# All nine groups of four output tiles by seven products: the last four plain tiles of a down-projection go

## The chip, the cores and the metric

One NeuronCore of a Trainium2 chip runs the kernel. The metric is the device time of one execution in microseconds (us). Engines are named as in the profile: PE is the matrix engine (PEld its weight loads), DVE the vector engine, ACT the scalar engine, POOL GpSimd, SP the sync engine, on whose queue nearly all transfers are issued.

## The reference

Attention with two kinds of windows for 8 batches of 8 heads, 576 positions of 64 values, followed by a two-layer projection with a leaky ReLU between:

```
scores = scale * q @ k^T                  # per batch and head
plain heads (0-3):    key in the last 32 positions
dilated heads (4-7):  key in the last 128 positions, every 4th
x = softmax(masked scores) @ v            # (8*576, 512) after merging the heads
h = x @ w_in                              # 512 -> 2048
g = max(0.01 * h, h)
out = g @ w_out                           # 2048 -> 512, (4608, 512) in fp32
```

## The kernel before

Operands are cast to fp16 and accumulated in fp32. The 4608 rows are worked in pairs of batches (1152 rows), each pair in three **chunks** of 384 rows. A chunk's up-projection makes 16 blocks of 128 hidden values, which ACT turns into `gt[c % 3]`. Chunk 0 belongs to batch 0, chunk 1 half to batch 0 and half to batch 1, chunk 2 to batch 1. The up-projection stands on line 1057 (blocks of 384 columns; ACT behind it on 1073), chunk 1's on line 1091 (two blocks of 192 at a time, its first half for batch 0 and its second for batch 1; ACT on 1104), and that of the last three chunks, by seven products, on line 1191.

Attention works in **visits** of two heads (dilated 2 and 3, then plain 0 and 1), two units each: scores (L899), exp on ACT (L907), sums (L924), values (L918), logarithm and reciprocal on ACT (L943, L945), normalisation on DVE into `xt` (L956). Batches 0 and 1 ("early") are loaded with long rows, cast, and transposed on PE (L743). What their first 512 positions leave over, 64 positions a head, is the **remainder**: loaded by `load_rest` into `rest`, transposed by PE (L791), and worked as a unit of its own (L993 to L1032). Batches 2 to 7 are loaded in 128-byte pieces, cast by POOL (L505), and transposed by DVE (L708, L713, L720).

The down-projection has 36 tiles of 128 rows by 512 columns. The first four (`PLAIN = 4`: the three of chunk 0 and the first of chunk 1) are plain: `down` makes each in four **parts** of four matmuls of 512 columns (L1271), evicts it with one copy (L1279) and stores it. A part needs four blocks of the chunk and four rows of `w_out`. The other 32 go through `group`, eight groups of four tiles. A group regards 2 x 2 pairs of tiles, halves of the hidden dimension and halves of the columns as a 2 x 2 block product and makes it of seven products (the Winograd form of Strassen's) instead of eight. One product is eight matmuls of 256 columns for each of two tiles (L1361). Before them DVE forms eight sums and differences of activations (`add_up`, L1347: s1 to s4, two tiles each, in the halves `rest` and `pair1` and in place in `gt`), and once for the whole kernel four of `w_out` (`weight_sums`, L1301: into the former staging buffer `wst`, into `t4`, and in place into `w_out`, this last one behind all plain parts). Between them ACT or DVE evicts or adds partial results (L1390, L1392, L1398). P1 and P2 use raw activations and raw weights only; the banks are `fps0`, `fps1` and `tp`, and the last group is split into more banks.

`w_in` comes in eight blocks of 512 KB (`w0` to `w7`) and `w_out` in another eight (`w8` to `w15`), staged in `gt[1]`, `gt[2]`, `wst` and `xt[1]`, and cast. The string `FIRST` gives the order of the first loads: `q01` is q and k of batch 0's heads 4 to 7, `v00` its v for heads 0 to 3, `r0` its remainder, `c` the mask table `con`.

All work is handed to a planner as tasks with engines, durations and dependences. It lists them by rank: `PASSES` passes of a forward list schedule and of latest starts. To the ranks of the best pass the table `NUDGE` adds a number by task, `HAND` fixes an engine by task, and a last forward pass gives the order in which instructions are emitted. Each engine then works its instructions in that order. `WHEN` gives first estimates of when a batch's attention starts; `ROOM`, `LATE`, `LANDS`, `SERVE`, `FSERVE`, `FAST` are the planner's figures for transfers; `SECOND` names the banks in which batch 1's transposes land. Up to the first up-projection, gaps in PE's plan are filled with idle matmuls (L1592).

Of the kernel before, what the change touches and what calls it, by code (L numbers as in the profile page):

```python
# [15 lines left out]
ROOM, LATE, LANDS, SERVE, FSERVE = 256, 1.06, 0.6, 1.1, 1.04  # L16
SOON = 0
FAST = 0.21
WHEN = (3.92, 2.82, 39.64, 80.18, 115.4, 117.81, 161.72, 152.03)
PASSES = 8  # L20
SEVEN = (9, 10, 11)
SECOND = 'st01t'
# [6 lines left out]
FIRST = ('r0 q01 q00 v01 v00 w0 w1 w2 w3 w4 w5 w6 q11 w7 w8 q10 w9 w10 v11 w11 w12 w13 w14 v10 '  # L29
         'w15 r1 c')  # L30
NUDGE = {
# [337 lines left out]
def kernel(  # L369
# [941 lines left out]
    def group(four, acts, at_time, split):  # L1311
# [67 lines left out]
        def w_raw(k, nn):  # L1379
            return lambda j: w_out[:, (k * HJ + j) * DM + nn * HN:(k * HJ + j) * DM + nn * HN + HN]  # L1380
# [278 lines left out]
```

## Time and profile before

| | |
|---|---|
| median of 3 runs | 294.5 us (294.27 to 294.89) |
| profiled execution | 294.39 us |
| its span, first to last instruction | 292.5 us |
| PE busy | 284.3 us (97%), granted clock 1.00 |
| DVE, ACT, POOL busy | 225.6, 218.5, 122.3 us |
| DMA | 47.15 MB, mean 161 GB/s |
| plain parts (L1271) | 64 matmuls, 37.8 to 74.1 us |
| seven products (L1361) | 896 matmuls, from 77.8 us |

How to read it: matmuls are pipelined, so the duration of one is its latency, and the pace is read from the chain of waits, which gives a run of matmuls with its length. A row of a table of windows gives, for a stretch of time, the busy time and number of instructions of each engine, the granted PE clock, the share of busy DMA engines and GB/s. A row of groups gives line, engine, operation, written tile and read tile, shapes and count, then busy time and mean, then the idle time before it and what ended it.

### The profile page before, as it was taken

To read this page: it belongs to the slowest core of one execution; us is meant where nothing else is said; L and a number is where in the kernel's file an instruction comes from. 1 tells how busy PE (TensorE), PEld (TensorE's weight loads), DVE (VectorE), ACT (ScalarE), POOL (GpSimd) and SP (SyncE) were. 2 spreads that over 40 slices of the span, in tenths; PEclk is the share of its full clock that TensorE was granted. 3 is DMA by queue.
4 is the path that set the end of the run, shared out by engine and by line. 5 is a ranking of instruction groups with operands and counts; after the bars stand their busy time and mean duration, and the time that the engine had idled before them with its cause. 6 is when DMAs were issued, how large, how long until landed. Compare 5 with 4: busy or idle time off the path is not lost.

```text
span 292.5 us, 7627 instructions
## 1 busy us (share of the span) xinstructions
PE 284.3 (97%) x2924; PEld 225.8 (77%) x2924; DVE 225.6 (77%) x437; ACT 218.5 (75%) x482; POOL 122.3 (42%) x174
## 2 busy tenths in 40 slices
PE   6889999999999999999999999999999999999995
PEld 2567776776787788677777877887688999999985
DVE  7967587674799789858839889897878889678672
ACT  4977987589869966878888987888767966755522
POOL 5440452458537746964863774653425000000000
PEclk9999999999999999999999999999999999999999
DMA  7999999699798978999898898831101210121133
GB/s 246 275 386 396 399 355 232 133 170 229 128 194 184 191 166 158 200 163 208 210 178 160 175 199 155 208 99 60 36 2 36 75 38 0 38 74 36 38 109 110
DMA packets 156068, 47.15 MB, mean 161 GB/s; under 512 B 136832, under 2 KB 153344, under 8 KB 156032
## 3 DMA queue, kind: packets, MB, share of 16 engines
q1 hardware_dynamic: 155344, 46.04, 65.0%
q10 hardware_dynamic: 688, 0.63, 0.6%
q8 instruction: 23, 0.38, 0.5%
q14 instruction: 13, 0.11, 0.1%
HBM read 37.22 MB, written 9.44 MB: 159 GB/s over the span
## 4 chain that ended last, share of the span: by engine, by line
PE 92%; DMA 3%; DVE 2%; ACT 1%; POOL 0%; issue 0%; ACTq 0%; SPq 0%; DVEq 0%
PE hps L1057 27%; PE fps L1361 23%; PE tp L1361 9%; PE hps L1191 5%; PE fps L1271 4%; PE hps L1091 4%; PE ops L1191 3%; PE ops L918 2%; DMA gt<-in_moe_w_in_dram 2%; PE ops L899 2%; PE ops L924 2%; PE sps L899 2%; PE sps L1191 1%; PE sps L924 1%; DMA con<-consts 1%; PE ops L1361 1%
## 5 line engine op out<-in xcount | busy, mean ns | idle before, releaser
L1057 PE MATMUL hps<-xt,w_in 128*128 128x384 f16 x488 | 94.7, 325 | 1.0 <-POOL w_in L505 1.0
L1361 PEld LDWEIGHTS <-gt 128*128 128x128 f16 x768 | 73.0, 98 | 9.8 <-DVE gt L1347 0.2
L1073 ACT ACTIVATE gt<-hps 128x384 f16<-128x384 f32 x122 | 59.2, 488 | 13.6 <-PE hps L1057 12.7
L1057 PEld LDWEIGHTS <-w_in 128*128 128x128 f16 x512 | 44.8, 98 | 22.5 <-POOL w_in L505 1.5
L505 POOL CAST slots<-vst 128x576 f16<-128x576 f32 x55 | 46.3, 867 | 23.0 <-DMA vst<-in_v_dram 5.6
L505 POOL CAST nat<-stg 128x576 f16<-128x576 f32 (+1 forms) x52 | 34.3, 681 | 48.3 <-DMA stg<-in_k_dram 23.6
L1361 PE MATMUL fps<-w_out,gt 128*128 128x256 f16 x368 | 46.7, 273 | 0.0
L911 DVE TENSOR_TENSOR ee<-ee,con 128x384 f16<-128x384 f16 (+1 forms) x48 | 20.6, 431 | 15.2 <-ACT ee L907 14.8
L945 ACT ACTIVATE rc<-rc 128x288 f32<-128x288 f32 (+1 forms) x64 | 27.2, 437 | 1.1
L956 DVE TENSOR_TENSOR xt<-ops,rc 128x288 f16<-128x288 f32 (+2 forms) x44 | 19.4, 446 | 10.4 <-ACT rc L945 5.5
L516 ACT COPY slots<-turned 64x512 f16<-64x512 f16 (+1 forms) x30 | 23.8, 800 | 0.8 <-DVE turned L708 0.5
L1214 ACT ACTIVATE gt<-vst 128x384 f16<-128x384 f32 (+1 forms) x24 | 16.0, 684 | 8.0 <-DVE vst L1210 8.0
L899 PEld LDWEIGHTS <-slots 128*128 128x128 f16 x308 | 18.1, 98 | 4.7 <-DVE slots L517 0.5
L517 POOL COPY slots<-turned 64x576 f16<-64x576 f16 (+2 forms) x25 | 16.7, 676 | 10.7 <-ACT slots L516 3.1
L907 ACT ACTIVATE ee<-ops 128x416 f16<-128x416 f32 (+2 forms) x35 | 16.7, 487 | 3.6 <-PE ops L899 3.0
L918 PEld LDWEIGHTS <-slots 128*128 128x128 f16 x308 | 17.1, 97 | 2.3 <-ACT slots L504 0.6
L924 PEld LDWEIGHTS <-con 128*128 128x128 f16 x168 | 14.0, 97 | 6.0 <-issue 1.0
L708 DVE STREAM_TRANSPOSE turned<-nat 128x576 f16<-128x576 f16 x24 | 18.0, 760 | 0.1
L1390 ACT COPY stg<-fps 128x512 f32<-128x512 f32 (+1 forms) x20 | 10.4, 520 | 9.4 <-PE fps L1361 9.0
L1347 DVE TENSOR_TENSOR gt<-gt 128x1024 f16<-128x1024 f16 x21 | 16.6, 792 | 0.3 <-PE fps L1361 0.2
L907 ACT ACTIVATE ee<-sps 128x416 f16<-128x416 f32 (+2 forms) x29 | 14.4, 497 | 3.2 <-PE sps L899 2.2
L1191 PEld LDWEIGHTS <-w_in 128*128 128x128 f16 x192 | 16.2, 98 | 0.3
(157 smaller groups left out, 557.8 us busy)
## 6 DMA issues: line engine op xcount, KB each, us to landing
out_dram<-osb SPq DMA_DIRECT2D x32, 256.0 KB, 2.7
stg<-in_k_dram SPq DMA_DIRECT2D x48, 144.0 KB, 3.7
stg<-in_q_dram SPq DMA_DIRECT2D x48, 144.0 KB, 3.4
vst<-in_v_dram SPq DMA_DIRECT2D x16, 288.0 KB, 4.2
vst<-in_v_dram SPq DMA_DIRECT2D x32, 128.0 KB, 3.2
gt<-in_moe_w_in_dram SPq DMA_DIRECT2D x6, 512.0 KB, 7.3
stg<-in_q_dram SPq DMA_DIRECT2D x3, 512.0 KB, 7.0
stg<-in_k_dram SPq DMA_DIRECT2D x3, 512.0 KB, 9.1
```

The costliest lines, as they stand in the source:

```text
L505: return ENG[e].tensor_copy(out=dst, in_=src)
L516: return nc.scalar.copy(out=dst, in_=src)
L899: nc.tensor.matmul(p_bank[:, c:c + w], slot(tn, KB + 128 * s, 0, 128, [1, 128]), slot(tn, qx, 0, 128, *qd), start=first or not by_pe, stop ...
L907: lambda e: nc.scalar.activation(out=et[:, 0:n], in_=p_bank[:, 0:n], func=AF.Exp, scale=SCALE), prio)
L911: lambda e: nc.vector.tensor_tensor(out=et[:, 0:n], in0=et[:, 0:n], in1=con[:, table:table + n], op=ALU.mult), prio,
L918: nc.tensor.matmul(at(dst, 0, 128, o, *od), lhs(s), et[:, c:c + w], start=i == 0, stop=i == len(steps) - 1, skip_group_check=True)
L924: nc.tensor.matmul(at(p_bank, 0, 128, o, *od), block_ones, at(et, 0, 128, c, *cd), start=i == 0, stop=i == len(rows) - 1, skip_group_check ...
L945: lambda e: nc.scalar.activation(out=rt, in_=rt, func=AF.Exp, scale=-1.0), prio)
L1057: nc.tensor.matmul(ht[:, 0:n], at(w_in, 0, 128, vi * DFF + j // 2 * 256 + j % 2, [2, 128]), at(xt[m % 2], 0, 128, vi * 1152 + x0 + x, [1, n]),
L1073: lambda e: nc.scalar.activation(out=gt[c % NG][:, j * n_c + x:j * n_c + x + n], in_=ht[:, 0:n], func=AF.Prelu, alpha=0.01),
L1191: nc.tensor.matmul(bk[:, n * i:n * i + n], w(v, 2 * z + i), x(v), start=first and i == 0 and v == 0, stop=i == 1 and v == 1, skip_group_ch ...
L1361: nc.tensor.matmul(bk[:, x:x + HN], tl[:, off + j * step:off + j * step + 128], rhs(j), start=first and x == 0 and j == 0, stop=j == HJ - ...
```

## The change

`PLAIN` becomes 0, so that tiles 0 to 3 form a ninth group, ahead of the eight, and no plain tile is left. P1 and P2 of each group get explicit dependences on the rows of `w_out` that they read. The order of the first loads, the bank of the first of batch 1's transposes, the planner's figures, and the whole tables `NUDGE` and `HAND` are new. The tables are left out here except for their ends.

```
-ROOM, LATE, LANDS, SERVE, FSERVE = 256, 1.06, 0.6, 1.1, 1.04
+ROOM, LATE, LANDS, SERVE, FSERVE = 256, 2.04, 0.6, 1.1, 1.04
-FAST = 0.21
-WHEN = (3.92, 2.82, 39.64, 80.18, 115.4, 117.81, 161.72, 152.03)
+FAST = 0.17
+WHEN = (2.79, 4.96, 47.9, 67.29, 111.55, 110.73, 171.21, 162.22)
-SECOND = 'st01t'
+SECOND = '1t01t'
-FIRST = ('r0 q01 q00 v01 v00 w0 w1 w2 w3 w4 w5 w6 q11 w7 w8 q10 w9 w10 v11 w11 w12 w13 w14 v10 '
+FIRST = ('v01 r0 q01 q00 v00 w0 w1 w2 w3 w4 w5 q11 w6 w7 q10 w8 v11 w9 w10 w11 v10 w12 w13 w14 '
          'w15 r1 c')
 NUDGE = {
-    1: 104.0, 2: -16.52, 3: -11.06, 4: 20.36, 5: 11.86, 9: 15.21, 11: 21.5, 20: 0.5, 21:
...
+    1: 106.5, 3: -2.56, 10: 64.75, 11: 3.9, 20: 1.98000000000002, 21: -0.5, 22: 0.494999999999891,
...
-    PLAIN = 4
+    PLAIN = 0
...
-        p1 = product(raw_of(0, 0), w_raw(0, 0), X, True, lambda i: ready(i, 0), 0, 0)
-        p2 = product(raw_of(0, 1), w_raw(1, 0), Y, True, lambda i: ready(i, 1), 1, 0)
+        rows_in = [sum((w_out_t[k * HJ + j] for j in range(HJ)), []) for k in range(2)]
+        p1 = product(raw_of(0, 0), w_raw(0, 0), X, True, lambda i: ready(i, 0) + rows_in[0], 0, 0)
+        p2 = product(raw_of(0, 1), w_raw(1, 0), Y, True, lambda i: ready(i, 1) + rows_in[1], 1, 0)
```

The ranks of the first loads are fixed by `FIRST` plus the `NUDGE` of their tasks. Worked out from both, they stand in this order (a load waits further where its buffer is not free yet; v loads of the heads 4 to 7, in six pieces, are given as `v01..` or `v11..` where their pieces stand together):

```
before: q01 (q) with r0, pieces of v01, q00, k00, v01.. and v00 whole,
        w0 w1 w2 w3 w7 w4 k11 w6 w5 w8 q11 k10 (v11) q10 w9 v11.. w10 w11 (w12) w13
        v10 second half, w14, v10 first half, w15, r1, con
after:  r0, q01 (q), pieces of v01, q00, k00, v00 second half, w0 w1, v00 first half,
        w2 w3 q11 k11 w6 w4 w5 w7 k10 q10 (v11) w8 v11.. w9 w11 w10
        v10 first half, w12 w15, v10 second half, w14 w13, r1, con
```

On ACT's queue, the load of the first constants stands behind batch 0's first k before, and ahead of it after.

More of the change, by code (lines that the diff above doesn't have):

```diff
@@ L28 @@
 STRETCH = 1.0
-FIRST = ('r0 q01 q00 v01 v00 w0 w1 w2 w3 w4 w5 w6 q11 w7 w8 q10 w9 w10 v11 w11 w12 w13 w14 v10 '
+FIRST = ('v01 r0 q01 q00 v00 w0 w1 w2 w3 w4 w5 q11 w6 w7 q10 w8 v11 w9 w10 w11 v10 w12 w13 w14 '
          'w15 r1 c')
 NUDGE = {
[78 rows of a table removed]
-HAND = {
-    2: "POOL", 3: "POOL", 9: "POOL", 36: "ACT", 37: "DVE", 59: "POOL", 89: "POOL", 91: "POOL", 92:
-    "POOL", 97: "POOL", 111: "POOL", 113: "POOL", 114: "POOL", 139: "DVE", 146: "ACT", 154: "DVE",
-    161: "DVE", 324: "ACT", 331: "DVE", 566: "POOL", 567: "ACT", 573: "DVE", 575: "DVE", 582:
-    "POOL", 727: "ACT", 729: "ACT", 737: "DVE", 892: "DVE", 1001: "POOL", 1004: "POOL", 1059:
-    "POOL", 1149: "ACT", 1167: "POOL", 1314: "DVE", 1322: "DVE", 1352: "DVE", 1588: "ACT", 1598:
-    "DVE", 1623: "POOL", 1629: "POOL", 1633: "ACT", 1728: "DVE", 1740: "DVE"}
[80 rows of a table added]
+HAND = {
+    2: "DVE", 3: "POOL", 5: "DVE", 11: "POOL", 44: "ACT", 47: "ACT", 51: "ACT", 53: "ACT", 55:
+    "POOL", 56: "POOL", 59: "POOL", 64: "POOL", 65: "POOL", 99: "POOL", 108: "POOL", 111: "POOL",
+    117: "POOL", 132: "POOL", 139: "DVE", 143: "DVE", 151: "DVE", 156: "DVE", 329: "DVE", 330:
+    "DVE", 342: "DVE", 484: "DVE", 487: "DVE", 577: "DVE", 584: "POOL", 591: "POOL", 743: "POOL",
+    745: "POOL", 749: "ACT", 939: "DVE", 949: "DVE", 999: "POOL", 1004: "POOL", 1009: "POOL", 1077:
+    "POOL", 1161: "POOL", 1171: "ACT", 1212: "POOL", 1419: "POOL", 1428: "POOL", 1552: "POOL", 1591:
+    "DVE", 1626: "ACT", 1632: "POOL", 1633: "ACT", 1634: "POOL", 1641: "ACT", 1678: "DVE", 1723:
+    "DVE", 1769: "DVE", 1789: "DVE", 1791: "DVE", 1805: "DVE", 1807: "ACT", 1837: "DVE", 1861:
+    "DVE", 1869: "DVE", 1876: "DVE"}
 HELD = 4
```

156 rows, old and new, of the table NUDGE are left out of this document.

## The prediction

> **What bounds the kernel now.** I read the page's shares first, then the table of 10 us windows, then the chain of waits.
>
> ```profile
> PE 284.3 (97%) x2924; PEld 225.8 (77%) x2924; DVE 225.6 (77%) x437; ACT 218.5 (75%) x482; POOL 122.3 (42%) x174
> 10.00:20.00 10.00, 7.88 (x90) 4.84 (x89) 8.06 (x17) 8.37 (x21) 5.04 (x7) 1.00 0.97 313
> 20.00:30.00 10.00, 10.00 (x133) 8.03 (x131) 7.56 (x21) 8.26 (x22) 0.62 (x1) 1.00 1.05 398
> 40.00:50.00 10.00, 9.70 (x112) 6.92 (x110) 7.20 (x16) 8.42 (x21) 3.24 (x5) 1.00 1.04 271
> 50.00:60.00 10.00, 10.00 (x128) 7.69 (x127) 7.11 (x16) 5.72 (x14) 3.10 (x4) 1.00 0.75 143
> 280.00:290.00 10.00, 9.58 (x88) 8.34 (x86) 5.39 (x11) 2.61 (x7) 0.00 (x0) 1.00 0.27 93
> ```
>
> The page gives PE 97% of the span. The windows (columns PE, PEld, DVE, ACT, POOL, clock, DMA share, GB/s) show where the rest is: PE is short of work up to 20 us, and then full to the last window. The DMA engines are saturated (share 0.97 to 1.05) until 50 us. So two things set the time: when PE first has enough to do, and how much it has to do after that. The profiled execution took 294.39 us for a span of 292.5, 0.1 below the median of 294.5; the sum is made against 294.39. About 0.2% (0.6 us) is what a measurement of this kernel can tell from no change.
>
> **Products instead of plain tiles.** The chain of waits gives the pace of each kind of product.
>
> ```profile
> 37.99 1.73 PE fps L1271 x8
> ...
> 87.44 1.75 PE fps L1361 x16
> ```
>
> Eight matmuls of 512 columns (the plain tiles, L1271) took 1.73 us, 0.216 each; sixteen of 256 columns (the sevens, L1361) took 1.75, 0.109 each. Four plain tiles are 4 x 16 = 64 wide matmuls, 13.8 us. A group is 7 products x 2 tiles x 8 = 112 narrow ones, 12.2 us. PE loses **1.6 us** of work. The 48 additional weight loads hide: the 1.75 us already contains sixteen.
>
> The page "TensorE: Matmul & The Clock Gate" of the Trainium skill (Back-to-back issue gap) speaks against such an exchange: it gives sustained spacings of about 81 ns at 128 columns and 131 ns at 512. By it the estimate is 64 x 131 ns = 8.4 us out against some 112 x 98 ns = 10.9 us in, 2.6 us lost. The two rows above disagree with it, and I give it no weight.
>
> The other engines get more work in the same place:
>
> ```profile
> L1279 DVE COPY osb<-fps 128x512 f32<-128x512 f32 x4 | 2.7, 684 | 0.0
> L1347 DVE TENSOR_TENSOR rest<-gt x8: 650/682/819, 80.2 to 278.0; 128x1024 f16<-128x1024 f16 x8
> L1398 DVE TENSOR_TENSOR osb<-fps,stg 128x512 f32<-128x512 f32 x7 | 4.7, 678 | 0.0
> L1390 ACT COPY stg<-fps 128x512 f32<-128x512 f32 x14 | 8.2, 583 | 2.9 <-PE fps L1361 2.5 <-DVE osb L1398 0.4
> ```
>
> Out go four copies of 0.68 on DVE (2.7 us). In come eight sums of 0.68 (5.5), three additions of 0.68 (2.0) on DVE, and four evictions of 0.58 (2.3), which ACT or DVE can take. DVE gains 4.8 us and ACT 2.3. In the windows 40 to 60 DVE has 5.7 us free and ACT 5.9, and the group may run on into the windows after that. I cost this at nothing by itself. The stores stay four of 128 x 512 elements; the fourth weight difference, now free of the plain tiles, only moves forward.
>
> **What can no longer fill PE early.** This is the expensive side.
>
> ```profile
> 37.00:51.00 14.00, 8.03 (x32) 2.66 (x32) 1.00 1.04 291
> 51.00:56.00 5.00, 3.94 (x16) 1.46 (x16) 1.00 0.71 115
> L505 DVE CAST w_out<-xt x4: 420/424/626, 29.1 to 47.4; 128x512 f16<-128x512 f32 x4
> L1301 DVE TENSOR_TENSOR wst<-w_out x1: 1409/1409/1409, 48.0 to 48.0; 128x2048 f16<-128x2048 f16 x1
> 51.02 0.39 PE L791 MATMUL tp<-con,rest 128*128 128x128 f16 x4
> 54.48 0.37 DVE L956 TENSOR_TENSOR xt<-sps,rc 128x224 f16<-128x224 f32 x1
> 55.93 1.48 PE L1091 MATMUL hps<-xt,w_in 128*128 128x192 f16 x16
> ```
>
> The first two rows are L1271 alone: between 37 and 51 us 32 matmuls, 32 x 0.216 = 6.9 us of PE work, and 16 more up to 56. A plain part needs only four rows of `w_out` and four blocks of the up-projection, so these fill PE while batch 1's attention is still under way. A group has only two products from raw operands (P1 with the first half of `w_out`, P2 with the second). The other five need the weight differences, which need all of `w_out` (last cast 47.4, first difference from 48.0), and sums of activations, of which one is built in `rest`, free only once batch 1's remainder has been transposed (L791, 51.02). So before 51 us there are at most 2 x 16 x 0.109 = 3.5 us of products. If nothing else moves up, **3.4 us** of PE time stays empty, more than the 1.6 saved. If enough moves up, nothing does. The nearest work is batch 1's own: its last normalisations stand at 54.48, and the second half of chunk 1 (64 matmuls on L1091) starts only behind them, at 55.93.
>
> **What the new load order moves.** SyncE's queue before:
>
> ```profile
> 11.50 2.87 SPq L489 DMA_DIRECT2D gt<-in_moe_w_in_dram  x4
> ...
> 37.93 0.61 SPq L489 DMA_DIRECT2D vst<-in_v_dram  x1
> 38.64 3.47 SPq L489 DMA_DIRECT2D xt<-in_moe_w_out_dram  x1
> 42.16 0.61 SPq L489 DMA_DIRECT2D stg<-in_q_dram  x1
> 42.81 0.63 SPq L489 DMA_DIRECT2D stg<-in_k_dram  x1
> 43.48 0.68 SPq L489 DMA_DIRECT2D con<-consts  x1
> gt<-in_moe_w_in_dram SPq DMA_DIRECT2D x6, 512.0 KB, 7.3
> vst<-in_v_dram SPq DMA_DIRECT2D x16, 288.0 KB, 4.2
> ```
>
> A 512 KB load takes 1.3 us at the 398 GB/s of the 20 to 30 window, one of 288 KB 0.7. The order worked out from `FIRST` and `NUDGE` reproduces this queue for before; for after it gives three moves. First, one 288 KB load of batch 0's v falls behind w0 and w1: the first weight block lands 0.7 us sooner. Second, q and k of batch 1's first half go ahead of the last four `w_in` blocks, and those of its second half ahead of all of `w_out`; the last `w_in` block lands about 1.3 later. Third, before, one 512 KB block of `w_out` followed batch 1's last v; after, two do. So batch 1's values are complete about 1.3 us earlier, and the last of `w_out` is no earlier, as the total is the same and the tail (remainder of batch 1, `con`) is the same.
>
> The start of PE's full stretch hangs on the first move:
>
> ```profile
> 11.50 6.08 DMA gt<-in_moe_w_in_dram
> 17.63 0.88 POOL w_in L505
> 18.55 0.34 PE hps L1057
> L505 DVE CAST w_in<-gt x9: 417/421/440, 17.6 to 28.2; 128x512 f16<-128x512 f32 x9
> ```
>
> The first weight block and its cast released the first up-projection at 18.55. The constants' lead on ACT's queue, which lets PE transpose sooner, is worth nothing while that cast ends last. Sooner by 0.7 at best; worse by up to 1.3 if the last `w_in` block (last cast 28.2 before) is then missed. Batch 1's transposes and chunk 1's first eight blocks cover that, and v for batch 0's plain heads comes later, so I take a gain of 0.3, with ends of -0.7 and +1.3.
>
> For the empty time I take 1.1 of 0 to 3.4: 1.3 us of earlier values brings batch 1's remaining attention and the first blocks of chunk 1's second half in front of 51 us, and the attention that stood between 51.02 and 55.93 moves with it: 4.9 us less 16 x 0.216 of plain parts is 1.4, of which I count 1.0, since the remainder's own unit stays behind. 3.4 - 1.3 - 1.0 = 1.1, an estimate.
>
> The added waits: P1 and P2 wait for whole halves of `w_out`. PE works in order, so everything ranked behind them stands too; where the ranks put them late enough they cost nothing, otherwise this is part of the 3.4. On SyncE's in-order queue the group's four stores come later than the plain ones; batch 2's loads, ranked between, start after `con` as before. The output stage at the end is unchanged.
>
> **Sum:** 294.39 - 1.6 + 1.1 - 0.3 = 293.6 against the profile, 293.7 against the median. I forecast **293.5**, a little under it: the hole is counted as if no part of chunk 1 but its first blocks moved up.
>
> **Rivals.**
> 1. *Early hole, slower.* The hole of 3.4 us stays: products wait for `w_out`, differences and `rest`, and batch 1 doesn't come forward because ACT is what holds it (8.42 of 10 us busy in 40 to 50). 294.39 - 1.6 + 3.4 = 296.2. It decides from a hole of 1.6 us on. For it: the 6.9 against 3.5 us. Against: DVE and POOL have room there to take casts and copies from ACT.
> 2. *No hole.* Batch 1 comes forward by all that is needed and the early weight block counts in full: 294.39 - 1.6 - 0.7 = 292.1. For it: the first half of batch 1's q and k moves ahead by several blocks.
> 3. *No change.* DVE's sums hold up POOL:
>
> ```profile
> POOL nat L505 <- DVE gt L1347: 15.1, 6, 3.9
> 55.27 3.10 POOL L505 CAST nat<-stg 128x576 f16<-128x576 f32 x4 [6.97 <-DMA stg<-in_k_dram]
> 87.96 0.42 DVE L956 TENSOR_TENSOR xt<-sps,rc 128x288 f16<-128x288 f32 x1
> 89.19 1.30 PE hps L1057 x8
> 90.49 0.87 PE fps L1361 x8
> 97.17 0.88 PE tp L1361 x8
> 98.70 0.87 PE tp L1361 x8
> ```
>
> POOL's casts waited up to 3.9 us for such sums. Group 0's now lie where batch 2's casts start (55.27). A 3.9 us delay there reaches its last normalisation (87.96) and chunk 3's start (89.19); the three products of group 1 left by then cover 2.6, so 1.3 is lost and the time is 294.39 - 1.6 + 1.3 = 294.1. The page "SBUF — State Buffer" of the Trainium skill (Who interferes with whom) says that a DVE instruction with two SBUF inputs and a GpSimd one that reads SBUF exclude each other; the first row agrees.
>
> **How the numbers follow.** Forecast 0.48 (292.8 to 294.2, of which 0.08 falls within 0.2%), hole 0.28, no hole 0.15, POOL 0.09. Faster by over 0.2% (under 293.9): 0.40 + 0.15 + 0.02 = 0.57. Within: 0.08 + 0.07 = 0.15. Slower (over 295.1): 0.28, the hole. The range 291.6 to 296.2 leaves out the ends of the second and first rival. As both signs hold weight, the forecast's own range, 292.8 to 294.2, stands beside it.
>
> **What would show it.** Right: no L1271, 1008 matmuls on L1361 at 0.109; PE full from about 20 us on except for some 1 us between 37 and 55; the second half of chunk 1 starting before 55; the last matmul about 1 us earlier than before. Wrong: PE at 8 or less in the windows 40 to 60, idle behind `w_out` casts or L1347 sums (rival 1); an idle PE near 88 behind an `xt` (rival 3); a last `w_in` cast after 30 us with PE waiting for it.

## The result

The changed kernel took 297.18 us (median of 4 runs, 296.91 to 297.94), the kernel before 294.69 (294.27 to 295.37) on the same chip: ratio 1.0084, interval 1.0061 to 1.0106. It is slower by 2.5 us. Forecast were 293.5 us, a range up to 296.2, and 0.28 for slower. The profiled execution took 296.91 us for a span of 294.8, 2.3 longer than before's 292.5. All line numbers of the changed kernel are higher by 5.

### The profile page after: what moved, and what is told of

Same layout as the page of the kernel before. It is cut to its first block, busy times and chain, and to the rows that moved or that the text cites. A ratio compares the mean times of both kernels' runs of the same rounds, so it can differ in the third digit from the quotient of the medians.

```text
span 294.8 us, 7724 instructions
## 1 busy us (share of the span) xinstructions
PE 283.9 (96%) x2968; PEld 231.2 (78%) x2968; DVE 221.3 (75%) x437; ACT 224.1 (76%) x493; POOL 127.4 (43%) x174
## 4 chain that ended last, share of the span: by engine, by line
PE 80%; DMA 9%; ACT 3%; SPq 3%; DVE 2%; POOL 1%; issue 1%; ACTq 0%
PE fps L1366 25%; PE hps L1062 23%; PE tp L1366 10%; DMA stg<-in_q_dram 6%; PE hps L1196 5%; PE ops L1196 3%; SPq L494 3%; PE ops L923 2%; PE hps L1096 2%; DMA gt<-in_moe_w_out_dram 2%; PE ops L904 2%; PE sps L1196 1%; PE ops L929 1%; PE sps L904 1%; PE sps L929 1%; DMA stg<-in_k_dram 1%
## 5 line engine op out<-in xcount | busy, mean ns | idle before, releaser
L1366 PEld LDWEIGHTS <-gt 128*128 128x128 f16 x864 | 81.0, 98 | 10.2
L510 POOL CAST slots<-vst 128x576 f16<-128x576 f32 x59 | 52.4, 913 | 28.6 <-DVE gt L1352 12.6
L510 POOL CAST nat<-stg 128x576 f16<-128x576 f32 (+1 forms) x50 | 36.8, 754 | 40.5 <-DVE gt L1352 18.1
L1366 PE MATMUL fps<-w_out,gt 128*128 128x256 f16 x416 | 52.4, 272 | 0.0
L521 ACT COPY slots<-turned 64x576 f16<-64x576 f16 (+1 forms) x35 | 28.2, 806 | 0.5
L950 ACT ACTIVATE rc<-rc 128x288 f32<-128x288 f32 (+2 forms) x64 | 27.3, 438 | 1.1
L1395 ACT COPY stg<-fps 128x512 f32<-128x512 f32 (+1 forms) x24 | 12.8, 534 | 15.0 <-PE fps L1366 9.8
L713 DVE STREAM_TRANSPOSE turned<-nat 128x576 f16<-128x576 f16 x24 | 18.1, 762 | 3.4 <-POOL nat L510 1.7
L1219 ACT ACTIVATE gt<-vst 128x768 f16<-128x768 f32 (+1 forms) x24 | 15.8, 681 | 6.2 <-DVE vst L1215 6.1
L1366 PE MATMUL fps<-wst,gt 128*128 128x256 f16 x144 | 18.5, 272 | 0.0
L1366 PE MATMUL tp<-w_out,gt 128*128 128x256 f16 x136 | 17.6, 272 | 0.0
```

What stands on the lines that cost most here:

```text
L510: return ENG[e].tensor_copy(out=dst, in_=src)
L521: return nc.scalar.copy(out=dst, in_=src)
L950: lambda e: nc.scalar.activation(out=rt, in_=rt, func=AF.Exp, scale=-1.0), prio)
L1366: nc.tensor.matmul(bk[:, x:x + HN], tl[:, off + j * step:off + j * step + 128], rhs(j), start=first and x == 0 and j == 0, stop=j == HJ - ...
```

## The profile after

First the page's shares, then the windows (PE, PEld, DVE, ACT, POOL, clock, DMA share, GB/s).

```profile
PE 283.9 (96%) x2968; PEld 231.2 (78%) x2968; DVE 221.3 (75%) x437; ACT 224.1 (76%) x493; POOL 127.4 (43%) x174
10.00:20.00 10.00, 7.42 (x92) 5.30 (x93) 6.94 (x14) 9.48 (x25) 5.05 (x8) 1.00 1.05 351
20.00:30.00 10.00, 9.58 (x131) 7.42 (x131) 6.92 (x18) 9.21 (x23) 4.33 (x8) 1.00 1.06 401
40.00:50.00 10.00, 9.54 (x131) 8.45 (x128) 6.66 (x16) 9.57 (x27) 3.93 (x5) 1.00 0.98 287
50.00:60.00 10.00, 9.77 (x134) 9.31 (x132) 10.00 (x17) 7.21 (x19) 4.01 (x1) 1.00 0.89 157
```

PE is never at 8 or less between 40 and 60 us, the mark that was set for an early hole. But DVE is at 10.00 between 50 and 60, where it stood at 7.11, and POOL works on a single instruction (x1) that is counted for 4.01 us. The page's chain of work that ended last (each step followed back to what released it, as shares of the span) has less of PE and more of the loads than before; first after, then before:

```profile
PE 80%; DMA 9%; ACT 3%; SPq 3%; DVE 2%; POOL 1%; issue 1%; ACTq 0%
PE 92%; DMA 3%; DVE 2%; ACT 1%; POOL 0%; issue 0%; ACTq 0%; SPq 0%; DVEq 0%
```

The next rows show PE with L1366 alone in two windows (PE, PEld, clock, DMA share, GB/s), then DVE, POOL and PE in order of time (start, duration, engine, line, operation, and in brackets the idle time with its releaser).

```profile
37.00:51.00 14.00, 3.62 (x31) 2.84 (x32) 1.00 0.98 284
51.00:56.00 5.00, 0.36 (x4) 0.08 (x1) 1.00 0.89 140
```

```profile
48.38 0.88 DVE L1352 TENSOR_TENSOR pair<-gt 128x1024 f16<-128x1024 f16 x1
...
53.73 1.21 DVE L1306 TENSOR_TENSOR wst<-w_out 128x2048 f16<-128x2048 f16 x1
...
58.21 1.21 DVE L1306 TENSOR_TENSOR t<-w_out,wst 128x2048 f16<-128x2048 f16 x1
59.35 0.68 DVE L1352 TENSOR_TENSOR gt<-gt 128x1024 f16<-128x1024 f16 x1
59.95 0.76 DVE L713 STREAM_TRANSPOSE turned<-nat 128x576 f16<-128x576 f16 x1
```

```profile
54.34 4.01 POOL L510 CAST nat<-stg 128x576 f16<-128x576 f32 x1 [5.61 <-DMA stg<-in_k_dram]
60.15 0.67 POOL L510 CAST nat<-stg 128x576 f16<-128x576 f32 x1 [1.81 <-DVE gt L1352]
```

```profile
66.53 0.34 PE L904 MATMUL sps<-slots 128*128 128x96 f16 x5
```

Against before:

```profile
58.95 1.43 DVE L708 STREAM_TRANSPOSE turned<-nat 128x576 f16<-128x576 f16 x2
64.20 0.34 PE L899 MATMUL sps<-slots 128*128 128x96 f16 x5
```

The 32 matmuls of P1 and P2 stand before 51 us, the 3.5 us that were counted. From 48 to 61 us DVE works without a break: the ninth group's eight sums and all four weight differences, and between them casts, normalisations and one transpose. Batch 2's second cast on POOL starts only at 60.15; before, its four casts stood in one row from 55.27 to 58.4. Batch 2's first scores on PE come at 66.53 instead of 64.20: 2.3 us later, as much as the whole span is longer.

## The experiments

Three theories. **H**: the new order of loads makes the head (up to 30 us) late. **F**: the plain parts filled early time on PE that nothing else can fill. **G**, formed after the first runs: the ninth group's sums on DVE hold POOL and with it batch 2. Beside every run before was run on the same chip; ratios are to it. Profiles are of single executions (at 30 us e1 stands 0.7 us sooner and e3 1.1 us later than before, though their order is the same up to there); ratios hold all runs.

### Nine groups in the old order, and plain tiles in the new one

In the first four (and in e6, f1, f2, g3 and g4 below) the planner's result is replaced by a written-out table of engine and place of every task; the numbers in it only give the order. It makes the line numbers of these kernels higher by some 1880.

e1_nine_old_order: before, with the ninth group. Every task that both kernels have keeps engine and place.

```
-NUDGE = {
...
+PLACE = {0: ('POOL', 1.4, 0.25),
...
+_Plan.run = _placed
...
-    PLAIN = 4
+    PLAIN = 0
```

> Nine groups, but every task that before also has keeps its engine and its place in that engine's order of before; only group 0 and the four weight differences are put in between. Theory H (the new order of the first loads and batch 0's later attention cost the time): the head is that of before, so 294.7 - 1.6 plus at most 0.5, 293.1 to 293.6 us. Theory F (the plain parts were the only thing that could fill PE between 37 and 56 us): slower than before even with the old head, 295.5 to 297.5 us, with the lost PE time between 40 and 60 us.

Measured: 298.18 us, ratio 1.0105 (1.0075 to 1.0134), a little above F's range. The products in two windows, below them the plain parts of before in nearly the same windows (count in brackets):

```profile
37.00:55.00 18.00, 4.12 (x32) 2.88 (x32) 1.00 0.99 250
55.00:79.00 24.00, 10.20 (x80) 7.62 (x80) 1.00 0.88 171
```

```profile
37.00:55.00 18.00, 11.45 (x47) 4.09 (x48) 1.00 0.98 252
55.00:77.00 22.00, 4.63 (x19) 1.56 (x17) 1.00 0.93 182
```

And the scores of batch 1's remainder on PE, first before, then here:

```profile
55.36 0.36 PE L993 MATMUL ops<-con 128*128 128x128 f16 x4
```

```profile
52.76 0.36 PE L2876 MATMUL ops<-con 128*128 128x128 f16 x4 [0.28 <-DVE xt L2839]
```

Up to 55 us 32 x 0.109 = 3.5 us of products replace 48 x 0.216 = 10.4 us of plain parts, 6.9 less, yet PE comes only 2.6 us sooner to the remainder. Behind 55 us 80 x 0.109 = 8.7 replace 16 x 0.216 = 3.5, 5.2 more. -2.6 + 5.2 = +2.6; from 80 us on the tasks that both kernels have stand 2.45 later here. So nine groups lose without any change of the loads: F's side is right, H's 293.1 to 293.6 is not.

e2_plain_new_order: after, with the plain tiles back, every task that both have in after's place (`PLAIN = 0` becomes 4, table as above).

> The four plain tiles are back, in the order of after: every common task keeps its place, the sixteen plain parts take places near those of group 0's products. Theory H: PE has 1.6 us more to do and the head of after, 297.2 to 298.8 us. Theory F: the parts fill PE early again, 294.7 to 296 us.

Measured: 298.71 us, ratio 1.0134 (1.0102 to 1.0165), within H's range. With plain tiles whole, after's order costs more (3.9 us) than the whole change. But that is not the loads alone. The plain parts stand near the places of the products, and so later than in before: the matmuls of plain parts (PE, PEld, clock, DMA share, GB/s) are

```profile
37.00:51.00 14.00, 4.16 (x17) 1.42 (x18) 1.00 0.98 311
51.00:56.00 5.00, 3.00 (x12) 0.87 (x12) 1.00 0.71 115
```

18 by 51 us where before had 32. What such a delay costs is the next run.

e3_plain_held: before, with four plain parts moved from before 51 us to behind 54 us and nothing else (four lines of the table on PE, with the evictions and stores behind them, such as these).

```
- 469: ('PE', 43.0392, 0.8633),
+ 469: ('PE', 49.629, 0.8633),
- 470: ('PE', 48.0901, 0.8633),
+ 470: ('PE', 52.8916, 0.8633),
```

> Before with its own order, only that four of the plain parts that ran before 51 us move behind 54 us and push the later ones back in turn, so that by 51 us PE has had 3.5 us of plain work, as much as a ninth group has to offer by then; nothing else is changed and the amount of work is the same. Theory F: +2 to +3.5 us, 296.7 to 298.2. Theory H: batch 1's attention moves up into the places, 294.7 to 295.3 us.

Measured: 297.61 us, ratio 1.0087 (1.0061 to 1.0112), as F gave it. In the profile, that of the slowest of its four executions, the common tasks fall back between 50 and 60 us from 0.44 to 3.88 us behind before: 3.4 of the 3.5 us (4 x 0.86) that were moved. Over all runs it is 0.87%, 2.6 us. Early filler that is moved behind 54 us is paid for by most of its length.

e4_rest_later: after, with batch 0's remainder moved in the loads behind the first unit's, and in the casts and transposes too.

```
+ 30: ('SP', 0.0, 0.65),
+ 31: ('SP', 1.3, 0.65),
+ 32: ('DVE', 8.7398, 0.2131),
...
```

> After, with only batch 0's remainder (its loads, casts, transposes and copies) moved behind the first unit's loads and copies, all other tasks in the places of after. Theory H, in the form that the remainder in front delays batch 0's first scores (11.44 us in after, 8.18 in before): first scores 1 us sooner and 296.3 to 296.8 us. If the first up-projections hang on the weight blocks all the same: 297.2 us, no change from after.

Measured: 297.83 us, ratio 1.01 (1.0074 to 1.0126): no gain, although batch 0's first scores come at 10.57 instead of 11.44. The place of the remainder in after's head isn't what costs it.

### Eight or nine groups, old or new loads

Four kernels without the tables `NUDGE` and `HAND` (the planner alone), with `PLAIN` 4 or 0, and with `FIRST`, `SECOND` and the planner's figures of before or of after. The edit of the first, and the further one of those with new loads:

```
-NUDGE = {
...
+NUDGE = {}
+HAND = {}
```

```
-FIRST = ('r0 q01 q00 v01 v00 w0 w1 w2 w3 w4 w5 w6 q11 w7 w8 q10 w9 w10 v11 w11 w12 w13 w14 v10 '
+FIRST = 'v01 r0 q01 q00 v00 w0 w1 w2 w3 w4 w5 q11 w6 w7 q10 w8 v11 w9 w10 w11 v10 w12 w13 w14 w15 r1 c'
...
```

> Before with NUDGE and HAND empty: eight groups, four plain tiles, the planner's own ranks, before's order of loads. One corner of a square of four (eight or nine groups, FIRST and planner's figures of before or of after), all with empty tables, so that no corner was made to fit. Expected 295 to 298 us. Theory F: the nine groups are slower by 1 to 3 us in both pairs, whatever the loads. Theory H: the structures differ by the 1.6 us of PE work, nine faster, and after's loads are slower by 1 to 2 us in both pairs.

> Nine groups, empty tables, before's FIRST and planner's figures. Theory F: 1 to 3 us above the eight groups with the same loads, the loss between 30 and 60 us. Theory H: 1 to 1.6 us below it.

> Eight groups and four plain tiles, empty tables, after's FIRST, SECOND and planner's figures. Theory F: about the time of the eight groups with the old loads, within 1 us. Theory H: 1 to 2 us above it, the loss up to 30 us.

> Nine groups, empty tables, after's FIRST, SECOND and planner's figures: after without its tables. Theory F: above the eight groups with the new loads by 0.5 to 2 us. Theory H: 1 to 1.6 us below them.

| | old loads | new loads |
|---|---|---|
| eight groups | 298.72 (1.015) | 299.58 (1.0173) |
| nine groups | 300.94 (1.0227) | 300.13 (1.0193) |

Nine groups cost 2.2 us more than eight with the old loads and 0.55 more with the new; H, which had them faster, is wrong in both pairs. The new loads cost eight groups 0.9 and give nine groups 0.8 back. The intervals are 0.3 to 0.5% (about 1 to 1.4 us) to either side, so only the first of the four differences stands by itself. The signs would fit a new order that is a remedy for part of what nine groups lose; these four runs don't show it.

### The load move in before

e6_qk_first: before, plain tiles kept; q and k of the first half of batch 1's heads 4 to 7 go ahead of the last four `w_in` blocks, with their casts and transposes. The table moves more than that: 8 of the 16 casts of `w_in` stand on POOL, as in after, where before has 3 there.

```
- 66: ('SP', 13.3591, 0.65),
+ 66: ('SP', 15.6534, 0.65),
- 69: ('SP', 16.9846, 0.65),
+ 69: ('SP', 19.647, 0.65),
...
```

> Before, plain tiles kept, with one of after's load moves alone: q and k of the first half of batch 1's heads 4 to 7 go ahead of the last four w_in blocks, and their casts, transposes and copies are moved with them; all other tasks keep engine and order. Theory H (the later weight blocks cost after its head): PE's real work by 30 us falls behind before's by 1 to 2 us, and as nothing regains it the time is 295.5 to 297. Theory F: the plain parts still fill 37 to 56 us, and work that comes later in the head is made up by them only if they have slack: they haven't, PE is full there, so a loss in the head would show whole under F as well; under F alone, without any cost of the loads, 294.5 to 295.2.

Measured: 297.23 us, ratio 1.0071 (1.0047 to 1.0095), 2.1 us. Two rows of the casts of `w_in` (first and last start behind the three durations), and PE in order of time:

```profile
L2380 DVE CAST w_in<-gt x6: 416/427/546, 16.8 to 31.4; 128x512 f16<-128x512 f32 x6
L2380 DVE CAST w_in<-wst x2: 408/418/427, 25.8 to 33.9; 128x512 f16<-128x512 f32 x2
31.82 0.50 PE L2932 MATMUL hps<-xt,w_in 128*128 128x384 f16 x2 [0.76 <-DVE w_in L2380]
```

The last cast of `w_in` starts at 33.9 instead of 28.2, PE waits for the one at 31.4, and the up-projection that stood at 29.89 starts at 31.82, 1.9 late. The lag stays at 1.9 to the end of the kernel. The chain to this up-projection (start, duration, what) shows that the cast stood in DVE's row behind a copy of batch 1's transposes:

```profile
31.01 0.42 DVE slots L2392
31.44 0.34 DVE w_in L2380
...
31.82 0.50 PE hps L2932 x2
```

The block itself had landed by the trace at 30.89, 3.1 us after the last one of before (27.79), so of the cast's delay the load explains all but the last 0.5 us. In after the last cast is at 31.1:

```profile
L510 DVE CAST w_in<-wst x2: 401/414/426, 25.6 to 31.1; 128x512 f16<-128x512 f32 x2
```

It is 2.9 later than before's (1.3 had been forecast for the load), but no wait of PE for it shows there. So e6 shows what such a move can cost, not that it costs the same in after.

### Tiles 0 to 3 cut to a quarter

c1_plain_quarter: before, with one matmul in each plain part instead of four. c2_group_quarter: after, with two of eight in each product of the ninth group. Tiles 0 to 3 are not computed whole then. The order of all that is left doesn't change.

```
-            for j in range(4 * p, 4 * p + 4):
+            for j in range(4 * p, 4 * p + 1):
...
```

```
-                    for j in range(HJ):
+                    for j in (range(HJ) if four[0] != (0, 0) else (0, HJ - 1)):
```

> Before, every engine's order unchanged, but each part of the four plain tiles makes one of its four matmuls (the other 48 are left out, so those four tiles are not computed whole): 48 x 0.216 = 10.4 us of PE work out, 36 of them (7.8 us) before 56 us and 12 (2.6 us) after 56 us. Theory F (early on, PE's work waits for loads, casts and batch 1's attention, and the plain parts only fill what would be empty): what is left out before 56 us is hardly got back, so the time falls by 2.6 to 6, to 289 to 292. Theory H (the plain parts are ordinary PE work, and after lost its time through its loads and its head): the time falls by the whole 10.4, to about 284.5.

> After, every engine's order unchanged, but each product of the ninth group (tiles 0 to 3) makes two of its eight matmuls for a tile (84 of 112 are left out, so those four tiles are not computed whole): 84 x 0.109 = 9.2 us of PE work out, 24 of them (2.6 us) before 51 us and 60 (6.5 us) from 57 us on, where PE is full. Theory F: the late 6.5 are got back whole and the early 2.6 hardly, so the time falls by 6 to 8, to 289.5 to 291.5; against the run before on the same chip this makes the ninth group and the plain tiles alike in what they fill, and the two shortened kernels should end within 2 us of each other although the plain one starts 2.4 us ahead. Theory H: all 9.2, to 288.

Measured: c1 293.23 us, ratio 0.9952 (0.9932 to 0.9972); c2 295.93, ratio 1.0036 (1.0018 to 1.0055). With 10.4 us of PE work out, before gains 1.4 us; with 9.2 out, after gains 1.4 (1.0084 - 1.0036 = 0.0048 of 294.4). F had expected 2.6 to 6 and 6 to 8, H everything: both are wrong, c2 worst, since 6.5 us of its work lay where PE is full. What holds c1 is in the chain that ended last (start, duration, what; "issue" is time in which the engine waited for nothing that the profile shows). In before it runs mostly over PE's plain parts there; here it runs over batch 1's attention on DVE and ACT up to the remainder, which PE reaches at 54.09 instead of 55.36:

```profile
47.88 0.69 ACT rc L943 x2
48.58 0.34 ACT rc L945
...
53.67 0.38 DVE xt L956
...
54.09 0.36 PE ops L993 x4
```

So 7.8 us of PE work less bring the remainder 1.3 us forward. PE back to back doesn't mean that PE alone sets the pace: the attention of batches 1 and 2 goes beside it at nearly the same pace, and an emptier PE hardly pulls it ahead. Batch 2's first scores stand at 64.55 in this profile (64.20 before), but that says less: it is the profile of c1's slowest execution (294.69 us), in which the clock fell behind 54 us (last section).

This also shows two floors, 293.2 and 295.9. What separates them isn't the work of tiles 0 to 3 on PE, of which 3.5 us are left in c1 and 3.1 in c2.

### Cut in both orders, and the sums cut too

f1_e1_group_quarter: e1 with c2's edit. f2_e2_plain_quarter: e2 with c1's edit.

> Nine groups in before's order, with each product of the ninth group cut to two of its eight matmuls for a tile (84 of 112 left out, so tiles 0 to 3 are not computed whole): 9.2 us of PE work out, 6.5 of them behind 55 us. The plain kernel cut in the same way fell to 293.2 and the changed kernel only to 295.9, so below the PE work each order has a floor of its own. Theory F: in before's order the nine groups lose time because 10 half-products of 0.87 (8.7 us) stand behind 55 us where 3.5 us of plain parts stood; cut to a quarter they are gone, and the time falls to the plain kernel's floor, 292.5 to 294.5. Rival G: the group's eight sums, its weight differences and its waits hold up the other engines in before's order too, and the time stays at 296 or more.

> Plain tiles in after's order, with each plain part cut to one of its four matmuls (48 of 64 left out, so tiles 0 to 3 are not computed whole): 10.4 us of PE work out. Theory H (after's order of loads and its head set a later floor, whatever stands in tiles 0 to 3): 295 to 296.5, as the changed kernel with its ninth group cut (295.9). If the floor of that kernel comes from the ninth group's sums and waits (rival G): 292.5 to 294, as before with the plain parts cut (293.2).

Measured: f1 296.30 us, ratio 1.0066 (1.0039 to 1.0092); f2 294.53, ratio 0.9998 (0.9983 to 1.0014). F is wrong for f1: with the products nearly gone, the nine groups in the old order still stand at 296. (Four of f1's seven executions show a mean clock of 0.988; the other three took 295.31, 295.49 and 296.30, so at the full clock its floor is nearer to 295.5.) f2 lies between the two values expected: with plain tiles, after's order has a floor 0.46% (1.35 us) above that of before's order. POOL in order of time in f1, and below it the chain that ended last, from two of the group's sums over POOL's cast to DVE's transpose:

```profile
59.58 2.50 POOL L2388 CAST nat<-stg 128x576 f16<-128x576 f32 x4 [11.48 <-DVE gt L3230]
```

```profile
58.17 1.30 DVE gt L3230 x2
...
59.58 0.68 POOL nat L2388
...
60.28 0.79 DVE turned L2591
```

Batch 2's four casts, at 55.27 before, start at 59.58 here, released by one of the group's sums. In c2 too the chain runs over DVE's row, from 50.80 to 60.64 with no other engine in it.

g2_small_sums_quarter: c2, and the ninth group's eight sums only over the two blocks that are still read. g4_e1_small_sums_quarter: the same in f1.

```
-            return at(g, 0, 128, k * HJ * n_c + x, [n_c, HJ], [1, 128])
+            return at(g, 0, 128, k * HJ * n_c + x,
+                      *([[n_c, HJ]] if four[0] != (0, 0) else [[n_c * (HJ - 1), 2]]), [1, 128])
...
```

> After, with the ninth group's products cut to two of eight matmuls for a tile as in the kernel that gave 295.9, and now also its eight DVE sums cut to the two blocks that those matmuls read (6 of 8 left out in each; tiles 0 to 3 are not computed whole). The weight differences, evictions and all waits stay. Theory G (between 48 and 61 us DVE's unbroken row of the ninth group's sums and weight differences holds POOL's casts of batch 2 and delays batch 2's transposes): 8 sums of 0.68 become about 0.25, some 3 us of DVE time go, batch 2's first scores come 1 to 1.5 us sooner and the time falls to 294.5, the value of after's order with plain parts cut. Theory H (the order of the loads and the head set the floor): no change, 295.9.

> Nine groups in before's order with the ninth group's products cut to two of eight matmuls (that gave 296.3), and now also its eight sums cut to two of eight blocks. Theory G: here DVE's row of sums stood from 54.7 to 59.9 us and POOL's casts of batch 2 waited behind it until 59.6; with the sums short they start about 2 us sooner and the time falls to 294 to 294.7, toward the 293.2 of the plain kernel cut in the same way. Theory H: this order's loads are before's, so H has no price here; if the time stays at 296, the weight differences or the evictions hold the chain, not the sums.

Measured: g2 294.15 us, ratio 1.0000 (0.998 to 1.002); g4 293.69, ratio 0.9987 (0.9971 to 1.0002). Taking three quarters of the sums away gives 0.36% (1.1 us) in after's order and 0.79% (2.3 us) in before's; both times are near those that G gave. In before's order part of it is the clock, which was lower in four of f1's runs: with the executions at the full clock alone, f1's median is 295.49 and g4's 293.65, against their befores 0.5%, 1.5 us. POOL and PE in order of time, first in g2, then in g4:

```profile
58.76 0.67 POOL L510 CAST nat<-stg 128x576 f16<-128x576 f32 x1 [2.25 <-DVE gt L1353]
65.01 0.34 PE L904 MATMUL sps<-slots 128*128 128x96 f16 x5
```

```profile
57.45 2.50 POOL L2388 CAST nat<-stg 128x576 f16<-128x576 f32 x4 [8.21 <-DVE gt L3231]
63.41 0.34 PE L2782 MATMUL sps<-slots 128*128 128x96 f16 x5
```

Batch 2's first scores come at 65.01 (67.16 in c2) and at 63.41 (65.53 in f1): 2.1 us sooner each time. In g2 the chain no longer runs over DVE's row between 51 and 60 us. From 70 us on all of PE stands 2.1 us sooner in g2 than in c2, and 2.1 to 2.5 in g4 than in f1. Part of that is the clock, which in the profiled runs of f1 (at 48 to 54 us) and c2 (at 64 to 66 us) fell to 0.50, and in these did not; the ratios hold all runs. g2 ends at f2's value (1.0000 and 0.9998): without its products and its sums the ninth group costs the same as plain parts cut as far.

g3_diff_later: after, whole, with the last weight difference behind batch 2's first transposes (one line of the table).

```
+ 463: ('DVE', 66.9732, 1.15),
```

> After, whole, with one move: the last weight difference (1.2 us on DVE, into the tile that only the group's last product reads, at 74 us) goes from before batch 2's first transposes behind its first masks, some 9 us later. Theory G with PE not quite full: batch 2's first transposes come 1.2 us sooner and the time falls by 0.5 to 1.2, to 296 to 296.7. Theory F (PE is full from 55 us on, so what comes sooner finds no room): 297.2, no change. If the difference now holds POOL's casts of batch 2 and its masks in turn: 297.5 to 299.

Measured: 297.63 us, ratio 1.0114 (1.0097 to 1.0131), no gain, and perhaps a loss (after 1.0084). The first transpose came at 58.59 (59.95 in after), the first scores only at 66.30 (66.53): PE was full in front of them, and in the profile of after the chain has no DVE between 47 and 70 us. That is F's argument, though the time lies in the third range expected. While the products are whole, PE's own row ends last there, and freeing 1.2 us of DVE gives nothing.

No version beat before. Not tried: `w_in` blocks first together with nine groups, and a buffer of its own for the sum that waits for `rest`. The sums cut with the products whole wasn't run either, so how the two share the loss in the whole kernel is known only in the one order of taking away; g3 says that there the sums stand second, behind PE's row.

## Why the prediction was wrong

**The sum as the runs give it.** From c1 by way of f2 and c2 to after, in ratios: after's order instead of before's, with plain parts cut, 0.9998 - 0.9952 = 0.46%, 1.35 us; the ninth group instead, cut, 1.0036 - 0.9998 = 0.38%, 1.1 us, which goes when its sums go; its products whole, 1.0084 - 1.0036 = 0.48%, 1.4 us. Back to before: plain parts whole instead of cut, 1 - 0.9952 = 0.48%, 1.4 us. 1.35 + 1.1 + 1.4 - 1.4 = 2.45, the 2.5 measured. Each term is uncertain by about 0.25% (0.8 us). The terms also hang on the way that is taken. By way of e2, with all work whole, after's order costs 3.9 us, with its plain parts placed late, and the products in their place give 1.5 back; by way of e1 the products cost 3.1 in before's order and the new order gives 0.6 back (within the noise). So order and products are not two prices that add up.

**The saved 1.6 us of PE work: counted right, but not a saving of time.** The matmuls are there at the pace forecast (32 by 51 us, 0.87 for eight). The step that failed comes first in the prediction: that after 20 us the time is set by "how much it has to do", read from windows at 10.00. c1 takes 10.4 us of that work away and gains 1.4 (1.9 at the full clock), because batch 1's attention on DVE and ACT ends hardly sooner. Up to 80 us the windows say that PE has something to do, not that the rest waits for it alone. Work that is moved to a later place there costs most of its length (e3: 2.6 to 3.4 of 3.5), taking it away brings little.

**The other engines' work "at nothing": 1.1 us.** The 5.5 us of sums were set against 5.7 us of free DVE time in the windows 40 to 60. But that time wasn't free for them: DVE's row from 48 to 61 stood in front of batch 2's transposes and in the way of POOL's casts. The 1.1 us is what the sums cost with the products cut (c2 against g2). Rival 3 had this mechanism (POOL held by the sums), and said that group 0's sums lie where batch 2's casts start. It then priced it by a delay at 88 us, where PE has no idle time in after, and gave it 0.09. The whole kernel's waits of POOL's casts for such sums hardly tell of it: 15.1 us before, 18.1 now, of which only 1.81 belong to batch 2 (60.15 above); the others end at 87, 116 and 135 us.

**The head: -0.3 taken, +1.35 measured for the whole order, and 2.1 for the load move with its casts in before (e6).** The end of the range on that side, 1.3, was near; the value taken was not. The 1.35 holds everything that the order moves, not the head alone; that the loads make it up is argued from e6 and from the greater share of DMA in after's chain, and not shown by itself. What was to cover the last `w_in` block, batch 1's transposes and chunk 1's first blocks, doesn't in e6. The first block did come sooner, nearly as forecast: its load is issued at 10.03 instead of 11.50, and the first cast of `w_in` on POOL starts at 16.85 instead of 17.63. But the first up-projection starts at 18.59 (18.55 before), directly behind four idle matmuls (17.73 to 18.59). So the gain of the first move was nothing.

**The hole: 1.1 of 0 to 3.4 taken.** Its arithmetic, 6.9 against 3.5 us, is what e1 shows in before's order, and rival 1's time, 296.2, is nearest to the result. But rival 1's mark, PE at 8 or less between 40 and 60, is not seen in after: batch 1 comes forward with the new order as forecast (chunk 1's second half from 51.42 instead of 55.93). Rival 1 was right on the side and wrong on the place: by the sum above the loss is in the new order and in DVE's row, and not in an empty PE between 40 and 60 us. Where in the new order its 1.35 us arise stays open.

## What to carry to other kernels

Before a saving on the busiest engine is counted, ask stage by stage whether another chain ends there at the same time: the cheapest test is to leave most of that work out with the order fixed, and here it gave 1.4 us for 10.4. Then follow the chain of that run: it names what ends next. Price the helper instructions of a cheaper algorithm at the place where they stand in their engine's row, by what is queued behind them, not by the free share of a window. Filler that needs few inputs is worth having where little else is ready: here 3.5 us of it, moved to a later place, cost 2.6 us. A replacement that needs all inputs moves work to such a place.

## What was not expected of the hardware

**The clock fell behind a short hole.** The granted clock in c1 in 2 us windows (PE, clock, DMA share, GB/s), where PE had just waited 1.85 us in one piece:

```profile
52.00:54.00 2.00, 0.24 (x2) 1.00 1.05 171
54.00:56.00 2.00, 1.91 (x28) 0.72 0.37 91
56.00:58.00 2.00, 2.00 (x17) 0.50 0.66 191
58.00:60.00 2.00, 2.00 (x35) 0.93 1.04 171
```

If the clock is 0.50 or 1.00 and nothing between, it was at half for (0.28 + 0.50 + 0.07) x 2 / 0.5 = 3.4 us, and PE lost half of that, 1.7 us. The page "TensorE: Matmul & The Clock Gate" of the Trainium skill (Part 1: The HAM clock gate) gives two states, half and full, and a window of about 3.4 us after which the gate changes; the length agrees. It puts the fall behind at least one idle window of that length; here it came behind a hole of 1.85 us. Of c1's ten executions three show a mean clock of 0.994 and took 294.07 to 294.69 us; the other seven, at 1.0, took 292.27 to 294.04, median 292.86. So at the full clock c1 gains 1.9 of 10.4 us, still far from the whole. That the hole is the cause was not tested by itself.

**One cast on POOL lasted 4.01 us** (L510 at 54.34 in after, 0.67 in most others) beside DVE's unbroken row of sums and weight differences, which have two inputs in SBUF. It ended at 58.35, 0.54 us behind the end of the last difference of that row (57.81). In g2 and g3 such a cast lasted 1.53 and 4.40 us and ended 0.5 us behind the end of the row too. The page "SBUF — State Buffer" of the Trainium skill (Who interferes with whom) says that a DVE instruction with two SBUF inputs and a GpSimd one that reads SBUF exclude each other; the traces agree. f1 and g4 show that the price is not the wait itself but the batch behind it.
